# A decode attention kernel with gated MLP: thirty of its 32 units become a loop of 15 rounds

## The chip, the cores and the metric

The kernel runs on one core of one Trainium2 chip. A core has five engines with instruction streams of their own: TensorE (PE; its weight loads are shown as PEld), VectorE (DVE), ScalarE (ACT), GpSimd (POOL) and SyncE (SP), which here issues nearly all DMAs. The engines meet at semaphores. Sixteen DMA engines move the data. The metric is the device time in microseconds (us); before the change it is 1358.99, the median of three runs from 1357.01 to 1359.01.

## The reference

One token for each of two batches (B = 2, D = 1024). Attention has 32 heads of size 128 and a cache of 16384 positions; the MLP has F = 3584. All is bf16.

```python
g = sigmoid((x * gate_w).sum(-1, keepdims=True))
q = (x @ wq)                                  # 32 heads of 128
p = softmax((q @ k_cache^T) * Dh ** -0.5)     # by batch and head, over 16384 positions
a = (p @ v_cache) @ wo
h = gelu(layernorm(x) @ w1)
hs = shifted(h) @ w2                          # four column groups, shifted along the sequence
x1 = x + hs
b = x1 + gelu(layernorm(x1) @ w3) @ w4
out = g * a + (1 - g) * b
```

With a sequence of length one every shifted group is zero, so hs is zero; w2 is multiplied all the same. K and V caches are 537 MB together, the weights 36 MB.

## The kernel before

A unit is a pair of heads of one batch: 32 units, in the order of head pairs with the two batches inside. The K rows of a unit are 128 partitions of 256 positions of 128 values, 8.39 MB; V the same. One SBUF tile, mem, has five cells of half a unit each. K of even units lies in cells 0 and 1, K of odd units in cells 1 and 2, V in cells 3 and 4 (only unit 30's V lies in cells 0 and 1). So the next K may be loaded when the half unit in the cell that both share has been used.

For a unit n the loop at L599, written out by Python, does this:

- score_first(n) and score_second(n): eight chunks. VectorE turns a chunk (L464, KT, two buffers), then TensorE multiplies it in eight matmuls (L470) with a sliding window of q (qw) into one PSUM bank S. score_first takes the four chunks of the shared cell.
- load_k(n + 1) (L97) stands between the halves.
- softmax_a and softmax_b: turn S, the maximum, the exponentials in two halves on ScalarE (L509) into pt, the sum and its reciprocal.
- pv(n - 2): 64 matmuls (L542) in four groups of rows, from pt and V into oacc. So V lags K by two units, with four pt tiles.
- load_v(n - 1) (L100), which waits for pv(n - 2) to free the V cells.
- pv_end(n - 2): ScalarE scales oacc into osb, four small matmuls (L560) add the groups up into OT; after both batches of a head pair, wo_project multiplies with wo (L432). wo comes four heads at a time (L425) in 2 KB rows.

SyncE takes the DMAs in program order, each with its waits in front of it. In the steady state one load moves while the next stands in the queue or waits.

The MLP lies inside units 0 and 1: w1 and w2 are loaded to cells 2 and 3, w3 into 3 and 4, w4 likewise, each when the weight or the K before it has been used. Its activations are held turned (LinearT: wide_bank at L210 and then small matmuls at L241 and L275 that turn the result).

At the end, the V of unit 31 comes in 11 pieces (load_v_pieces, L108), so that pv_last can begin early: the first pieces as in pv, the rest position by position with V as the weights (L587). load_probes (L447) issues six tiny DMAs from gate_w into a tile that nothing reads; they write the same tile, so that each waits until the one before has landed, and they stand in SyncE's stream between the last loads of K and V. The result row goes out in two halves by the queues of SyncE and ScalarE.

Of the kernel before, what the change touches and what calls it, by code (L numbers as in the profile page):

```python
# [23 lines left out]
def kernel(  # L24
# [26 lines left out]

# [11 lines left out]
    assert NJ % CT == 0 and CT % GT == 0 and NG <= QP  # L63
# [3 lines left out]
    wopool = ctx.enter_context(tc.tile_pool(name="wopool", bufs=1))  # L67
# [3 lines left out]
    sps = ctx.enter_context(tc.tile_pool(name="sps", bufs=2, space=PSUM))  # L71
    ops = ctx.enter_context(tc.tile_pool(name="ops", bufs=1, space=PSUM))
    rps = ctx.enter_context(tc.tile_pool(name="rps", bufs=1, space=PSUM))
# [8 lines left out]
    def region(cell, elements):  # L82
        return mem[:, cell * CELL : cell * CELL + elements]

    k_cell = [0 if u % 2 == 0 else 1 for u in range(NU)]
    v_cell = [3] * NU
    v_cell[NU - 2] = 0
    units = [(hp, b) for hp in range(HP) for b in range(B)]

    def cache_rows(cache, u):  # L90
        hp, b = units[u]
        return cache[b, 2 * hp : 2 * hp + 2].rearrange("h s d -> (h s) d").rearrange(
            "(p j) d -> p (j d)", p=P
        )

    def load_k(u):
        nc.sync.dma_start(out=region(k_cell[u], NJ * Dh), in_=cache_rows(A_k_cache, u))  # L97

    def load_v(u):
        nc.sync.dma_start(out=region(v_cell[u], NJ * Dh), in_=cache_rows(A_v_cache, u))  # L100

    PIECES = [32] * 6 + [16] * 3 + [8] * 2
    assert sum(PIECES) == NJ

    def load_v_pieces(u):
        j = 0
        for n in PIECES:
            nc.sync.dma_start(  # L108
                out=region(v_cell[u], NJ * Dh)[:, j * Dh : (j + n) * Dh],
                in_=cache_rows(A_v_cache, u)[:, j * Dh : (j + n) * Dh],  # L110
            )
            j += n

    def k_view(u):
        return region(k_cell[u], NJ * Dh).rearrange("p (j d) -> p j d", d=Dh)

    def v_view(u):
        return region(v_cell[u], NJ * Dh).rearrange("p (j d) -> p j d", d=Dh)

    wq_t = region(3, KC * H * Dh).rearrange("p (r n) -> p r n", r=KC)  # L120
    nc.sync.dma_start(out=region(3, KC * H * Dh), in_=A_wq.rearrange("(p r) n -> p (r n)", p=P))
    xin = const.tile([P, B, KC], BF16)
    nc.sync.dma_start(out=xin[:], in_=A_x.rearrange("b s (p r) -> p (b s) r", p=P))
    gwT = const.tile([P, KC], BF16)
    nc.sync.dma_start(out=gwT[:], in_=gate_w.rearrange("(p r) -> p r", p=P))
    load_k(0)
# [12 lines left out]
    sel = const.tile([P, 4, Q4, QP], BF16)  # L139
    nc.gpsimd.memset(sel[:], 0.0)  # L140
    for v in range(4):
        w, e = divmod(v, 2)
        nc.gpsimd.affine_select(
            out=sel[:, v],
            in_=sel[:, v],
            compare_op=ALU.not_equal,
            fill=1.0,
            base=-(2 * QP * w + e),
            pattern=[[0, Q4], [-2, QP]],
            channel_multiplier=1,  # L150
        )
# [9 lines left out]
    )  # L161

# [11 lines left out]
    sel8 = const.tile([P, 8], FP32)  # L174
    nc.vector.tensor_reduce(
        out=sel8[:],
        in_=ident_f[:].rearrange("p (c k) -> p k c", k=QP)[:, 0:8, :],
        axis=AX.X,
        op=ALU.add,
    )  # L180
    oacc = [ops.tile([P, 4 * Dh], FP32, name=f"oacc{k}") for k in range(2)]
    for k in range(2):
        nc.vector.memset(oacc[k][:], 0.0)

    NW = 2
    WW = P + NG
    qw = []
    for k in range(NW):
        t = const.tile([P, 4, WW], BF16, name=f"qw{k}")
        nc.gpsimd.memset(t[:], 0.0)  # L190
        qw.append(t)
    NP = 4
    pts = []
    for k in range(NP):
        t = const.tile([P, NJ // 4, 2, 4], BF16, name=f"pt{k}")
        nc.gpsimd.memset(t[:], 0.0)
        pts.append(t)

    def copy_bank(j, dst, src):
        if j % 2 == 0:  # L200
            nc.scalar.activation(out=dst, in_=src, func=ACTF.Copy)  # L201
        else:
            nc.vector.tensor_copy(out=dst, in_=src)  # L203

    def wide_bank(j, actT, weight, R, dst):

        acc = oacc[j % 2]
        for r in range(R):
            q = r % Q4
            nc.tensor.matmul(  # L210
                acc[QP * q : QP * q + B, :],
                lhsT=actT[:, r, :],
                rhs=weight[:, r, :],
                start=(r < Q4),
                stop=(r >= R - Q4),
            )
        copy_bank(j, dst, acc[:])

    class LinearT:

        def __init__(self, W, actT, name, cell, offset):
            self.actT = actT
            K, self.N = W.shape
            self.R = K // P
            self.C = self.N // P
            self.src = W.rearrange("(p r) n -> p (r n)", p=P)
            at = cell * CELL + offset
            self.dst = mem[:, at : at + self.R * self.N]
            self.acc = mlp.tile([P, self.C, B], FP32, name=f"{name}_acc")

        def load(self):
            nc.sync.dma_start(out=self.dst, in_=self.src)

        def compute(self, wide):
            wc = self.dst.rearrange("p (r n) -> p r n", n=self.N)
            for j in range(self.N // 512):
                at = slice(j * 512, (j + 1) * 512)
                wide_bank(j, self.actT, wc[:, :, at], self.R, wide[:, at])
            ps = misc_psum([P, self.C, B])
            for c in range(self.C):  # L240
                nc.tensor.matmul(  # L241
                    ps[:, c, :],
                    lhsT=wide.rearrange("p (m c) -> p c m", c=self.C)[:, c, :],
                    rhs=sel8[:, 0:B],
                    start=True,
                    stop=True,
                )
            nc.vector.tensor_copy(out=self.acc[:], in_=ps[:])

    xn1T = mlp.tile([P, KC, B], BF16)  # L250
    hT = mlp.tile([P, KC, B], BF16)
    shT = mlp.tile([P, KC, B], BF16)
    x1T = mlp.tile([P, KC, B], FP32)
    xn2T = mlp.tile([P, KC, B], BF16)
    h2T = mlp.tile([P, FC, B], BF16)
    bT = mlp.tile([P, KC, B], FP32)

    lin1 = LinearT(B_w1, xn1T, "w1", 2, 0)
    lin2 = LinearT(B_w2, shT, "w2", 2, KC * D)
    lin3 = LinearT(B_w3, xn2T, "w3", 3, 0)  # L260
    lin4 = LinearT(B_w4, h2T, "w4", 3, 0)
    lin1.load()
    lin2.load()
# [3 lines left out]

    qps = misc_psum([P, H, B])
    HB = 512 // Dh
    qwide = mlp.tile([P, D], FP32, tag="wide", name="wide")[:].rearrange("p (t n) -> p t n", t=2)  # L270
    for j in range(H // HB):
        qo = qwide[:, j % 2]
        wide_bank(j, xT, wq_t[:, :, j * 512 : (j + 1) * 512], KC, qo)
        for k in range(HB):
            nc.tensor.matmul(  # L275
                qps[:, j * HB + k, :],
                lhsT=qo[:, k * Dh : (k + 1) * Dh],
                rhs=sel8[:, 0:B],
                start=True,
                stop=True,  # L280
            )
    lin3.load()
    qT = const.tile([P, H, B], BF16)
    nc.vector.tensor_copy(out=qT[:], in_=qps[:])
    qdps = misc_psum([P, 4, H * B])
    for v in range(4):
        nc.tensor.matmul(
            qdps[:, v, :],
            lhsT=sel[:, v].rearrange("p a k -> p (a k)"),
            rhs=qT[:].rearrange("p h b -> p (h b)"),  # L290
            start=True,
            stop=True,
        )

    qd = const.tile([P, HP, B, 4], BF16)
    for e in range(2):
        rows = slice(e * HALF, (e + 1) * HALF)
        nc.vector.tensor_copy(
            out=qd[rows],
            in_=qdps[rows].rearrange("p v (hp e b) -> p hp e b v", e=2, b=B)[:, :, e],  # L300
        )
    qdu = qd[:].rearrange("p hp b v -> p (hp b) v")

    def write_qw(u):
        t = qw[u % NW]
        dst = t[:, :, NG - 1 : NG - 1 + QP * (Q4 - 1) + 1 : QP]
        nc.gpsimd.tensor_tensor(  # L307
            out=dst,
            in0=qdu[:, u, :].unsqueeze(2).to_broadcast([P, 4, Q4]),
            in1=mask4[:].unsqueeze(1).to_broadcast([P, 4, Q4]),  # L310
            op=ALU.mult,
        )

    g_rep = const.tile([P, B], FP32)

    def compute_gate():
        xg = mlp.tile([P, B, KC], FP32, name="xg")
        nc.vector.tensor_tensor(
            out=xg[:], in0=xin[:], in1=gwT[:].unsqueeze(1).to_broadcast([P, B, KC]), op=ALU.mult
# [57 lines left out]
    def wide4():  # L377
        return mlp.tile([P, D], FP32, tag="wide", name="wide")[:]
# [298 lines left out]
```

## Time and profile before

| what | value |
|---|---|
| three runs, us | 1357.01 to 1359.01, median 1358.99 |
| profiled execution, first to last instruction, us | 1358.0 |
| bytes read from HBM | 572.53 MB, 422 GB/s over the span |
| mean granted TensorE clock | 0.785 |
| K or V of one unit | 8.39 MB, 64 such in all |
| VectorE turning K chunks (L464) | 571.4 us in 256 instructions of 2.28 us |
| TensorE scores (L470) | 551.9 us in 2048 matmuls |

A window's line has its start and end, its length, then busy time and number of instructions of PE, PEld, DVE, ACT and POOL, then the granted clock, the share of the 16 DMA engines' time that packets took, and GB/s; packets are counted where they start. In the table of SyncE's waits, a line names the issuing line, who released it, the total, how often, and the longest. In the timeline a row has start and length, engine, line, operation and tiles, how many, and in brackets the idle time before it and who ended it. SPq marks an instruction of SyncE's stream that issues a DMA.

### The profile page before, as it was taken

Reading aid. Unit: us, or ns where it says so; the run is one execution under the profiler, and the core shown is the slowest. Engines: PE = TensorE matmul, PEld = TensorE weight load, DVE = VectorE, ACT = ScalarE, POOL = GpSimd, SP = SyncE. Lnnn points to the kernel's source line nnn. Section 1 sums busy time; section 2 is a strip of 40 time slices with the busy share of each in tenths; the row PEclk is TensorE's granted clock in tenths of the full one; section 3 lists DMA queues with packets and bytes.
Section 4 is the critical chain, followed back from the end, with each engine's and each line's share of the span. In section 5 each row is a group of like instructions: output and inputs, shape, how many; then the busy total and the mean of one; then the engine's idle time right before and its main releaser. Section 6 shows DMA issues by size and latency. Waiting matters only on the chain.

```text
span 1358.0 us, 11505 instructions
## 1 busy us (share of the span) xinstructions
PE 806.9 (59%) x5086; PEld 366.8 (27%) x5086; DVE 650.4 (48%) x511; ACT 133.5 (10%) x208; POOL 15.2 (1%) x54
## 2 busy tenths in 40 slices
PE   2897855555665545566555556655456665555564
PEld 1463422222222222222222222222222222222222
DVE  1436654444555534455544445555344555444450
ACT  0011011111100111110011111001111100111110
POOL 1000000000000000000000000000000000000000
PEclk9977877778876768888777788877678886777886
DMA  9987999999999999999999999999999999999996
GB/s 402 433 360 315 431 433 433 431 431 427 433 433 432 424 438 433 435 435 426 436 433 433 431 429 433 431 431 428 433 431 429 433 427 432 435 435 435 425 424 277
DMA packets 16183, 573.26 MB, mean 422 GB/s; under 512 B 1922, under 2 KB 1926, under 8 KB 6662
## 3 DMA queue, kind: packets, MB, share of 16 engines
q1 hardware_dynamic: 16130, 572.54, 98.1%
q8 instruction: 39, 0.64, 0.2%
q14 instruction: 10, 0.08, 0.0%
q10 hardware_dynamic: 4, 0.00, 0.0%
HBM read 572.53 MB, written 0.00 MB: 422 GB/s over the span
## 4 chain that ended last, share of the span: by engine, by line
DMA 67%; PE 17%; DVE 12%; issue 3%; ACT 0%; SPq 0%; POOL 0%; DVEq 0%; ACTq 0%
DMA mem<-in_A_k_cache_dram 57%; PE S L470 12%; DVE KT L464 11%; DMA probe<-in_gate_w_dram 7%; PE misc L241 2%; DMA xin<-in_A_x_dram 2%; PE oacc L210 1%; PE misc L275 1%; DMA wo<-in_A_wo_dram 1%; DMA mem<-in_A_v_cache_dram 0%; PE oacc L542 0%; PE arow L409 0%; ACT pt L509 0%; ACT mem L201 0%; DVE wide L203 0%
## 5 line engine op out<-in xcount | busy, mean ns | idle before, releaser
L470 PE MATMUL S<-KT,qw 128*128 128x512 bf16 x2048 | 551.9, 420 | 385.0 <-DVE KT L464 384.6
L464 DVE STREAM_TRANSPOSE KT<-mem 128x2048 f32<-128x2048 f32 x256 | 571.4, 2283 | 297.3 <-DMA mem<-in_A_k_cache_dram 243.6
L470 PEld LDWEIGHTS <-qw 128*128 128x128 bf16 x2048 | 219.8, 108 | 711.0 <-issue 537.0
L542 PE MATMUL oacc<-mem,pt 128*8 128x512 bf16 x2008 | 115.5, 382 | 8.6 <-DMA mem<-in_A_v_cache_dram 8.6
L495 ACT ACTIVATE Dm<-ident_s,m 128x128 f32<-128x128 f32 x32 | 12.8, 401 | 983.6 <-DVE m L493 983.6
L509 ACT ACTIVATE pt<-St,nb 64x256 bf16<-64x256 f32 x64 | 89.7, 1402 | 73.3 <-DVE nb L507 65.7
L572 DVE TENSOR_SCALAR OT<-misc,g_rep 128x2 bf16<-128x2 f32 x31 | 6.9, 222 | 140.5 <-PE misc L560 140.5
L520 PE MATMUL misc<-rs,lmat 128*128 128x1 f32 x62 | 17.8, 356 | 87.0 <-ACT pt L509 87.0
L542 PEld LDWEIGHTS <-pt 128*8 128x8 bf16 x2008 | 46.2, 87 | 74.5 <-issue 23.6
L522 DVE RECIPROCAL rinv<-misc 128x1 f32<-128x1 f32 x31 | 5.2, 168 | 101.6 <-PE misc L520 101.6
L491 DVE STREAM_TRANSPOSE St<-S 128x512 f32<-128x512 f32 x32 | 22.9, 717 | 63.7 <-PE S L470 63.7
L560 PE MATMUL misc<-sel,osb 128*128 128x2 f32 x256 | 34.5, 257 | 26.7 <-ACT osb L555 26.7
L560 PEld LDWEIGHTS misc<-sel,osb 128*128 128x128 f32 x256 | 31.8, 195 | 42.9 <-ACT osb L555 42.9
L520 PEld LDWEIGHTS misc<-rs,lmat 128*128 128x128 f32 x62 | 15.1, 303 | 97.9 <-ACT pt L509 97.7
L509 ACT ACTIVATION_READ_ACCUMULATOR pt<-St,nb 64x1 f32 x64 | 30.6, 478 | 0.0
L555 ACT ACTIVATE osb<-oacc,rinv 128x512 f32<-128x512 f32 x31 | 21.3, 687 | 69.0 <-PE oacc L542 69.0
L210 PE MATMUL oacc<-mem,xT 128*2 128x512 bf16 x64 | 9.4, 612 | 24.0 <-DVE xT L266 23.2
L307 POOL TENSOR_TENSOR qw<-qd,mask 128x16 bf16<-128x16 bf16 x32 | 8.4, 266 | 1180.9 <-PE S L470 1137.3
L507 DVE TENSOR_REDUCE nb<-misc 64x1 f32<-64x64 f32 x64 | 14.2, 222 | 5.0 <-PE misc L501 0.9
L275 PEld LDWEIGHTS misc<-sel,wide 128*128 128x128 f32 x64 | 14.2, 328 | 7.4 <-issue 4.4
L203 DVE COPY wide<-oacc 128x512 f32<-128x512 f32 x7 | 4.8, 691 | 22.9 <-PE oacc L210 22.9
L501 PE MATMUL misc<-Dm,ones_f 128*128 128x128 f32 x64 | 15.6, 326 | 0.0
(96 smaller groups left out, 168.3 us busy)
## 6 DMA issues: line engine op xcount, KB each, us to landing
mem<-in_B_w_dram SPq DMA_DIRECT2D x2, 7168.0 KB, 25.0
wo<-in_A_wo_dram SPq DMA_DIRECT2D x7, 1024.0 KB, 32.8
mem<-in_A_v_cache_dram SPq DMA_DIRECT2D x6, 1024.0 KB, 5.9
mem<-in_B_w_dram SPq DMA_DIRECT2D x2, 2048.0 KB, 45.9
mem<-in_A_v_cache_dram SPq DMA_DIRECT2D x3, 512.0 KB, 14.3
wo<-in_A_wo_dram SPq DMA_DIRECT2D x2, 512.0 KB
mem<-in_A_k_cache_dram SPq DMA_DIRECT2D x32, 28.2
mem<-in_A_v_cache_dram SPq DMA_DIRECT2D x2, 256.0 KB, 14.0
```

The source lines that it names most:

```text
L210: nc.tensor.matmul(acc[QP * q : QP * q + B, :], lhsT=actT[:, r, :], rhs=weight[:, r, :], start=(r < Q4), stop=(r >= R - Q4),)
L241: nc.tensor.matmul(ps[:, c, :], lhsT=wide.rearrange("p (m c) -> p c m", c=self.C)[:, c, :], rhs=sel8[:, 0:B], start=True, stop=True,)
L275: nc.tensor.matmul(qps[:, j * HB + k, :], lhsT=qo[:, k * Dh : (k + 1) * Dh], rhs=sel8[:, 0:B], start=True, stop=True,)
L464: nc.vector.transpose(out=kt[:], in_=Kc.rearrange("p j d -> p (j d)").bitcast(FP32))
L470: nc.tensor.matmul(S, lhsT=t[:, v, NG - 1 - m : NG - 1 - m + P], rhs=ktb[:, half * GT : (half + 1) * GT, w, :, e], start=(first and n == 0 ...
L491: nc.vector.transpose(out=st[:].rearrange("p j r -> p (j r)"), in_=S[:])
L501: nc.tensor.matmul(R_ps[:], lhsT=ones_f[:], rhs=Dm[:], start=True, stop=True)
L509: nc.scalar.activation(out=Pt[rows, :, e, :].rearrange("p (m a) k -> p a k m", a=GT // 4), in_=st[rows, :, 0:NG].rearrange("p (a k) m -> p ...
L520: nc.tensor.matmul(tot_ps[:, 0:1], lhsT=lmat[:], rhs=rs[:], start=True, stop=True)
L542: nc.tensor.matmul(acc[QP * q : QP * q + 8, :], lhsT=pts[u % NP][:, g].rearrange("p h k -> p (h k)"), rhs=v_view(u)[:, 4 * g : 4 * g + 4, ...
L555: nc.scalar.activation(out=osb[:], in_=oacc[u % 2][:], func=ACTF.Copy, scale=rinvs[u % NP][:, 0:1] if scaled else 1.0,)
L560: nc.tensor.matmul(ot[:], lhsT=osb[:, k * Dh : (k + 1) * Dh], rhs=sel8[:, k : k + 5 : 4], start=(k == 0), stop=(last and k == 3),)
```

## The change

1. The MLP comes first, ahead of the scores, with w1, w2, w3 and wq loaded at once into free cells, K of unit 0 after w3 has been used, and w4 in V's cells. x and gate_w are loaded by ScalarE's queue. The matmuls of the MLP and of q run as four column groups (rows4), and VectorE turns the results.
2. V lags K by one unit, so that two pt tiles suffice: K(n + 1), V(n), K(n + 2), V(n + 1).
3. wo is loaded and multiplied by head pairs (load_wo, project), 4 KB a row; pv_end sums into the layout that fits it, in sixteen small matmuls. arow takes one PSUM bank in four row groups.
4. The probes go. The last V comes in five pieces, and into cells 0 and 1.
5. Units 1 to 30 become a hardware loop of 15 rounds (from the second half of an odd unit to the first half of the next one). The addresses of the loads come from the loop's register. Its semaphores are not set back between rounds; they grow, and the waits compare with registers that grow by the same amount every round. The last unit stands in a branch inside the loop that only round 14 takes. The instruction order shows what the other rounds run instead: an arm that adds to each engine's and each load's semaphore what the last unit would have added. Before each such addition stands a wait for the count that the semaphore must have by then. On SyncE these are the counts of the round's two K loads, two V loads and the wo pair.

```diff
+    xin = const.tile([P, B, KC], BF16)
+    nc.scalar.dma_start(out=xin[:], in_=A_x.rearrange("b s (p r) -> p (b s) r", p=P))
...
+    w1 = load_weight(B_w1, 0)
+    w2 = load_weight(B_w2, 0, KC * D)
+    w3 = load_weight(B_w3, 1)
+    wq = load_weight(A_wq, 3)
+
+    K_CELL = (0, 1)
+    V_CELL = 3
+
+    def cache_rows(cache, hp, b):
+        two = cache[b, bass.ds(2 * hp, 2)]
+        return two.rearrange("h s d -> (h s) d").rearrange("(p j) d -> p (j d)", p=P)
...
+    def rows4(acc, actT, weight, R, at, n, G):
         for r in range(R):
+            for g in range(Q4):
+                nc.tensor.matmul(
+                    acc[QP * g : QP * g + B, 0:n],
+                    lhsT=actT[:, r, :],
+                    rhs=weight[:, r, g * G + at : g * G + at + n],
+                    start=(r == 0),
+                    stop=(r == R - 1),
                 )
...
+    def load_wo(hp):
+        rows = A_wo[bass.ds(hp * 2 * Dh, 2 * Dh)]
+        nc.sync.dma_start(
+            out=wo_pair[:].rearrange("p t n -> p (t n)"),
+            in_=rows.rearrange("(p t) n -> p (t n)", p=P),
+        )
+
+    def project(oT, weight, last):
+        for t in range(2):
+            for g in range(Q4):
+                nc.tensor.matmul(
+                    arow[QP * g : QP * g + B, :],
+                    lhsT=oT[:, t, :],
+                    rhs=weight[:, t, g * G1 : (g + 1) * G1],
...
-    def load_probes():
-        for n, pitch, width in (
-            (17, 60, 20), (2, 512, 30), (4, 256, 40), (8, 128, 50), (11, 93, 60), (13, 78, 70),
-        ):
...
+    def pv_end(b):
+        osb = pv_rows(b, True)[:].rearrange("p (k d t) -> p k t d", k=4, t=2)
+        ot = misc_psum([P, 2])
+        for t in range(2):
+            for k in range(4):
+                for h in range(2):
+                    nc.tensor.matmul(
+                        ot[h * HALF : (h + 1) * HALF, t : t + 1],
+                        lhsT=osb[:, k, t, :],
+                        rhs=lane[:, k + 4 * h : k + 4 * h + 1],
...
+    PIECES = (128, 64, 32, 16, 16)
...
+    load_k(0, 0)
+    w4 = load_weight(B_w4, 3)
+    score_first(0, 0)
+    load_k(0, 1)
+    score_second(0)
+    softmax_a(0)
+    mlp_last(w4)
+    load_v(0, 0)
+    softmax_b(0)
+
+    def odd_rest(hp):
+        load_k(hp + 1, 0)
+        score_second(1)
+        softmax_a(1)
+        pv(0)
+        load_v(hp, 1)
+        pv_end(0)
+        softmax_b(1)
+
+    def even_unit(hp):
+        score_first(hp, 0)
+        load_k(hp, 1)
+        score_second(0)
+        softmax_a(0)
+        pv(1)
+        load_v(hp, 0)
+        pv_end(1)
+        project(oT, wo_pair, False)
+        load_wo(hp)
+        softmax_b(0)
+        score_first(hp, 1)
+
+    load_wo(0)
+    score_first(0, 1)
+
+    def last_unit(hp):
+        V_LAST = 0
+        load_v(hp, 1, V_LAST, PIECES)
+        score_second(1)
+        wo_last = region(V_CELL, 2 * D).rearrange("p (h n) -> p h n", h=2)
+        softmax_a(1)
+        pv(0)
+        pv_end_apart(0)
+        nc.sync.dma_start(
+            out=wo_last, in_=A_wo[(H - 2) * Dh : H * Dh].rearrange("(h d) n -> d h n", d=Dh)
+        )
+        softmax_b(1, by_head=True)
+        pv_last(1, V_LAST)
+        project(OTl, wo_last, True)
...
+        with tc.For_i(0, HP - 1, 1, iteration_sync="reg_based") as i:
+            odd_rest(i)
+            even_unit(i + 1)
+            with tc.If(i >= HP - 2):
+                last_unit(HP - 1)
```

## The prediction

> **What bounds the kernel now.** I read four views. First the page: engines at half load, DMA at nine tenths in nearly every slice.
>
> ```profile
> PE 806.9 (59%) x5086; PEld 366.8 (27%) x5086; DVE 650.4 (48%) x511; ACT 133.5 (10%) x208; POOL 15.2 (1%) x54
> DMA  9987999999999999999999999999999999999996
> GB/s 402 433 360 315 431 433 433 431 431 427 433 433 432 424 438 433 435 435 426 436 433 433 431 429 433 431 431 428 433 431 429 433 427 432 435 435 435 425 424 277
> ```
>
> So time is bytes over rate plus the places where the stream breaks. Second the windows (last two columns: share of the 16 DMA engines, GB/s), which price the breaks:
>
> ```profile
> 0.00:140.00 140.00, 98.45 (x522) 59.60 (x522) 53.51 (x80) 11.93 (x21) 7.76 (x26) 0.88 0.89 375
> 140.00:1320.00 1180.00, 691.91 (x4296) 296.66 (x4295) 595.25 (x425) 118.21 (x182) 7.47 (x28) 0.78 1.00 432
> 1320.00:1340.00 20.00, 8.41 (x99) 3.91 (x99) 0.85 (x4) 2.77 (x6) 0.00 (x0) 0.67 0.77 313
> ...
> 68.00:70.00 2.00, 2.00 (x10) 2.00 (x10) 0.92 (x1) 0.00 (x0) 0.00 (x0) 0.95 0.04 8
> 70.00:72.50 2.50, 2.50 (x15) 1.07 (x15) 0.89 (x3) 0.60 (x1) 0.00 (x0) 0.50 0.00 0
> 72.50:75.00 2.50, 2.50 (x7) 0.81 (x6) 0.24 (x2) 0.00 (x0) 0.00 (x0) 0.50 1.29 419
> ...
> 114.00:122.50 8.50, 7.86 (x28) 2.92 (x27) 7.03 (x4) 0.00 (x0) 0.00 (x0) 0.79 0.00 0
> ```
>
> From 140 to 1320 us the stream never breaks: 432 GB/s. It breaks at the start (first packet at 1.8), near 70 and 114 us (the queue runs dry) and in the last 38 us. Third, SyncE's waits: K's load waits for the transposes that free its half cell, and the probes wait for each other.
>
> ```profile
> SPq L97 <- DVE KT L464: 351.8, 31, 28.5
> SPq L447 <- DMA probe<-in_gate_w_dram: 36.3, 5, 14.6
> ```
>
> Fourth the timeline, one unit and the first dry spot: how long after K has landed the next K is issued (11.2 us; the V behind it moves for 19.4), and how soon after an issue bytes flow (issue 71.72, above nothing until 72.5).
>
> ```profile
> 1249.59 4.50 DVE L464 STREAM_TRANSPOSE KT<-mem 128x2048 f32<-128x2048 f32 x2 [7.74 <-DMA mem<-in_A_k_cache_dram]
> ...
> 1260.74 0.33 SPq L97 DMA_DIRECT2D mem<-in_A_k_cache_dram  x1
> ...
> 71.72 0.33 SPq L97 DMA_DIRECT2D mem<-in_A_k_cache_dram  x1
> ```
>
> **The change, part by part.** One K or V load is 8.39 MB, so 19.4 us at 432 GB/s.
>
> Front. The breaks at 70 and 114 us come from K loads that wait for MLP work. 0 to 140 us at 375 instead of 432 GB/s costs 140 x (1 - 375/432) = 18.5 us; of it the start keeps 1.8 idle and 0.95 for slow first packets (first 64 KB packets took about 3.2 us, later ones 2.42, and began up to 0.2 apart): 2.7. The new order loads w1, w2, w3, wq (19.9 MB, done near 49 us) with x and gate_w on ACT's own queue. Work in that cover: gate and layer norm took 48.2 to 52.7 us here, 4.5 us; two small layers with gelu about 10; w3's 64 matmuls, in 16 groups at the cold 0.43 us, 7. From w3's landing near 29 us this ends by 37, and K0 is not due before 49. The rest: w4 waits for wq's matmuls (49 + 7 = 56, due 68); K1 for 11.2 us after K0 (80, due 85); V0 for w4's 112 matmuls after unit 0's scores (about 96, due 104); K2 for unit 1's first half (about 118, due 124). Nothing breaks: -15.8 us. If x came late behind weight packets, K0 still has 12 us of cover. Of the front's matmuls none is on the path.
>
> Probes. 1320 to 1340 us at 313 GB/s costs 5.5, by the DMA share of 0.77 4.6: the last V pieces stand behind probes that wait for their predecessor to land. The probes go: -5. The end after the last packet (1353.45 to 1358.0) stays, with the same piece matmuls, projection, copy and store; leaving the loop adds a wait row and a barrier on each engine, +1 (0.4 to 2; the barrier rows at the end of this trace last 0.6).
>
> wo. Heads 30 and 31 are loaded twice (as a pair in round 14, then apart): 0.52 MB, +1.2 us. Pairs come as 4 KB rows. Each single-buffered pair waits for its predecessor's projection, which ends some 10 us after the V load ahead of it starts; that V covers it. The eight matmuls of a projection are spread over 15 rounds, PE idle 41%: nothing. Sixteen small fp32 matmuls a unit replace four, which are eight rows of 0.12 us here (0.97 us a unit): 3 us more of PE. After the odd unit's V that makes 7 for pv, 1 for the copy, 4, 1 for the projection and about 5 of softmax, 18 us, ahead of the next K at 19.4; a few us late would only use up the 6 that PE has before the drain. Nothing, but this is the thinnest cover.
>
> K and V in turn. V(n) now follows K(n+1) and not K(n+2); pv(n) reads it one unit later. V's cell must be free 19.4 us after pv's data landed. In the order of the changed kernel pv of the even unit is mixed with the second score half: from V's landing 3.6 us of pv (64 matmuls), 32 score matmuls at 0.24, a cold start: 14 us. The odd unit's pv stands after all eight chunks: about 26 us after K, 7 after V landed. Both have 5 to 10 us left: nothing, and if that cover fell short by a microsecond it would cost 15.
>
> The loop. Semaphores are counted so that every round adds the same, whether or not the arm of the last round ran. In the rounds that skip it an else-arm makes up the counts, and each engine first waits for its own counts. PE, DVE and ACT wait for what they have done anyway. SyncE's arm, as the built order shows, waits for the landing of every load of the round, V and wo pair too, and only then may it pass on to the next round's K. Before, that K was issued with a V still moving (1260.74 above). So in 14 rounds (the last takes the true arm) the DMA queue runs empty: V, wo pair, nothing behind.
>
> What does one drain cost? Idle: from the last packet to SyncE's next issue 0.65 us (five probes: 0.52 to 0.75 from their last packet to the next issue); about 14 sequencer instructions of SyncE between (rest of the arm, two branches, counters, five waits) at 0.06 us, the spacing of the met waits at this trace's end: 0.84; from issue to first packet 0.97 (71.72 to 72.69; 121.69 to 122.66). Sum 2.5. Edges: the 18.5 us above less 13.0 idle (1.8, 2.67 from 70.02 to 72.69, 8.51) leave 5.5 for three slow starts of 0.95 and two run-outs, in which some of the 16 engines finish up to 1.9 us before the last: 1.3 each. One drain has one of both: 2.3. Together 4.8 us, and 14 drains 67 us. Loop branches and waits on registers are not in this trace. Low: 0.5 + 0.4 + 0.9 idle, edges 1.5, so 3.3. High: four of the 14 as long as SyncE's longest row, 0.5, idle 4.0, edges 2.7 as near 70 us, so 6.7. I take 4.8: the two dry spots are the same event. 14 drains: 46 to 94 us.
>
> The Trainium skill ("DMA: Bandwidth & Descriptors", Anatomy of one DMA) gives each transfer about 2.0 us that do not scale with its bytes. By it 14 drains would be 28 us and the time 1368; the dry spot near 70 us, 2.67 us idle and some 2 more in edges, speaks for more.
>
> Sum against the profiled execution: 1358.0 - 15.8 - 5 + 1.2 + 1 + 67 = 1406.4. The median of the runs, 1358.99, is 1.0 above that span, so 1407.
>
> **Rivals.** (1) Faster: the drain is nearly free. Without it the sum is 1358.0 - 15.8 - 5 + 2.2 + 1 = 1340. It decides at (1359 - 1340)/14 = 1.3 us a round: under that the kernel is faster. For it: the last load of a round is small (0.5 MB), and if its packets filled the gaps of engines that finish early, the run-out would vanish. Against: issue to first packet alone is 0.97 and the notice 0.5. Time 1345 to 1359. (2) A light drain, 1.3 to 3.3 us: 1359 to 1386. (3) The edge costs more: SyncE's jumps over the true arm and back wait for code. A tiny transfer's full round (stores issued 1355.6, waited for until 1356.98) is 1.3 us, an 8 KB code packet took 0.3 to 0.55; some 1.9 a jump, two a round: 14 x 3.8 = 53 more, 1460. For it: every other part of the loop is new. Against: SyncE's loop is some 70 instructions, less than one such packet. The Trainium skill ("Runtime: NRT & Kernel Launch", Instruction fetch mechanics) has a taken branch out of the fetched window wait for its page; no loop runs in this trace. For PE, whose round is nearly 600 instructions and whose jump skips 450 more, stalls of up to 6 us hide before the V it waits for, 10 more behind the next K. (4) Compute becomes late: pv after V's landing takes over 20 instead of 14 us, or the chain of small matmuls holds up the next scores, and SyncE waits for PE in each round; each microsecond costs 15: 1420 to 1450. Against: the 10 us left.
>
> **How the numbers follow.** Forecast (3.3 to 6.7 a drain) 0.78; (1) 0.05; (2) 0.06; (3) 0.06; (4) 0.05. Likeliest 1407. The forecast's own range is 1386 to 1434; with 3 us for the front and tail, and reaching into (3) and (4), 1383 to 1440. A measurement here can tell about 0.2%, 2.7 us. Only (1) is not slower: faster 0.04, same 0.01, slower 0.95.
>
> **What would show it.** Right: the DMA row between 5 and 1330 us has 14 dry spots of 2 to 4 us, some 80 to 85 us apart, each after a wo pair's landing and ended by a K issue; none before 120 us; SyncE's longest waits name V or wo landings at the loop's end; 432 GB/s between. Wrong: no dry spots (1), spots of 1 us (2), spots over 5 us (3), K or V issues released by PE with the queue empty (4), or a dry spot before 120 us (front).

## The result and the profile after

The changed kernel takes 1401.1 us (median of four runs, 1400.64 to 1401.93) against 1359.0 for the kernel before on the same chip (1357.01 to 1359.68): a ratio of 1.0315, 95% interval 1.030 to 1.033. The profiled execution took 1400.64 us, its span is 1398.5. The forecast was 1407.

The page of the changed kernel: its span, the DMA and GB/s rows in 40 slices of 35 us, and the queue that fetches code.

```profile
span 1398.5 us, 14865 instructions
DMA  9999989989899998999989999998999999998995
GB/s 420 396 442 432 428 376 442 427 375 444 381 422 427 396 450 375 429 396 420 450 375 441 384 420 405 420 450 375 424 399 422 403 422 420 405 420 379 446 420 241
q8 instruction: 8, 0.13, 0.0%
```

The hole near 110 us is gone; instead slices of 375 to 396 GB/s recur to the end. The windows put prices on it (last columns: granted clock, DMA share, GB/s):

```profile
0.00:140.00 140.00, 58.54 (x571) 26.36 (x575) 52.97 (x83) 8.07 (x15) 5.34 (x19) 0.83 0.99 422
140.00:1320.00 1180.00, 695.97 (x4798) 289.56 (x4787) 572.82 (x403) 112.99 (x174) 7.49 (x28) 0.78 0.96 413
1320.00:1384.00 64.00, 37.93 (x288) 15.65 (x289) 26.08 (x24) 7.79 (x12) 0.00 (x0) 0.78 1.00 426
1384.00:1398.50 14.50, 7.09 (x115) 4.14 (x107) 0.59 (x2) 0.60 (x1) 0.00 (x0) 0.62 0.01 2
```

The front went from 375 to 422 GB/s. The long middle went from 432 to 413: 1180 x (1 - 413/431.9) = 52 us. And the kernel now runs 14 us on after its last large packet, where before it ran 4.5.

The middle holds 14 dry spots, the first at 207.30 us, the others 82.3 to 82.9 us apart, each of 2.62 to 2.74 us without any packet. The first one, 206 to 212 us in 40 slices of 0.15 us (packets are counted where they start):

```profile
DMA  4444332000000000000000000099990999000000
GB/s 164 191 191 164 164 137 82 27 0 0 0 0 0 0 0 0 0 0 0 0 0 0 0 0 0 0 2621 437 1748 437 0 437 874 437 0 0 0 0 0 0
```

The small packets at the left are the rows of the wo pair; the large ones at the right are the next round's K, issued by SyncE 1.73 us after the last packet of wo (timeline):

```profile
209.03 0.33 SPq L108 DMA_DIRECT2D mem<-in_A_k_cache_dram  x1
```

SyncE's waits name the place: L632 is the branch that holds the last unit; 42 waits are three in each of 14 rounds. The table names the branch itself as the releaser, because each of these instructions raises the semaphore that it waits for. Which landing ends each wait shows in the trace's times: in the first round the three waits end at 187.1, 206.5 and 207.7 us, each within 0.05 us of the last landing of the round's second K, its second V and its wo pair. Only what follows the last of them stops the stream; the two before run while data still moves.

```profile
SPq L632 <- SPq L632: 413.6, 42, 19.4
```

The end of the kernel, TensorE from 1352 us on and then the last burst:

```profile
1353.53 1.90 PE L426 MATMUL S<-KT,qw 128*128 128x512 bf16 x8 [0.30 <-DVE KT L420]
1362.38 1.87 PE L492 MATMUL oacc<-mem,pt 128*8 128x512 bf16 x13 [6.95 <-DMA mem<-in_A_v_cache_dram]
1364.17 4.62 PE L426 MATMUL S<-KT,qw 128*128 128x512 bf16 x16
...
1389.02 2.30 PEld L548 LDWEIGHTS <-mem 128*128 128x128 bf16 x64
1389.13 2.27 PE L548 MATMUL misc<-pt,mem 128*128 128x2 bf16 x64
1393.15 0.16 DVE L552 TENSOR_TENSOR OTl<-misc,rinv 128x2 bf16<-128x2 f32 x1 [10.07 <-remote]
```

TensorE stands still for 6.95 us for the V of the other batch (pv(0)) while scores of the last unit that could run are queued behind it. And VectorE starts 1.75 us after the last matmul of the burst has ended. Neither was in the prediction.

Theories. T1: the else-arm's wait for landings on SyncE empties the DMA queue in 14 rounds, and that is the whole loss in the middle. T2: the loop's machinery as such costs it (branches, waits against registers, a semaphore raise on each TensorE instruction). T3, narrower: branch and arm cost the time whatever they wait for. For the end: the order of TensorE's work in the last unit.

### The profile page after: what moved, and what is told of

Same layout as the page of the kernel before. It is cut to its first block, busy times and chain, and to the rows that moved or that the text cites. A ratio compares the mean times of both kernels' runs of the same rounds, so it can differ in the third digit from the quotient of the medians.

```text
span 1398.5 us, 14865 instructions
## 1 busy us (share of the span) xinstructions
PE 799.5 (57%) x5758; PEld 335.7 (24%) x5758; DVE 652.5 (47%) x511; ACT 129.4 (9%) x202; POOL 12.8 (1%) x47
## 2 busy tenths in 40 slices
DMA packets 13529, 573.20 MB, mean 410 GB/s; under 512 B 1864, under 2 KB 1872, under 8 KB 4432
## 5 line engine op out<-in xcount | busy, mean ns | idle before, releaser
L426 PE MATMUL S<-KT,qw 128*128 128x512 bf16 x2048 | 564.8, 429 | 301.6 <-DVE KT L420 295.1
L492 PE MATMUL oacc<-mem,pt 128*8 128x512 bf16 x2032 | 146.0, 408 | 113.8 <-SPq L632 96.3
L492 PEld LDWEIGHTS <-pt 128*8 128x8 bf16 x2032 | 50.1, 88 | 197.1 <-issue 153.4
L525 DVE TENSOR_SCALAR oT<-misc,g_rep 128x2 bf16<-128x2 f32 x30 | 6.7, 222 | 120.2 <-PE misc L517 120.2
L517 PE MATMUL misc<-lane,osb 128*64 128x1 f32 x960 | 33.8, 199 | 39.4 <-ACT osb L505 39.4
L517 PEld LDWEIGHTS misc<-lane,osb 128*64 128x64 f32 x960 | 31.7, 138 | 54.1 <-ACT osb L505 28.1
L357 POOL TENSOR_TENSOR qw<-qdu,mask 128x16 bf16<-128x16 bf16 x32 | 8.5, 267 | 1239.9 <-PE L492 1165.2
L462 DVE TENSOR_REDUCE nb<-misc 64x1 f32<-64x64 f32 x64 | 14.2, 222 | 9.3 <-PE misc L457 5.2
L449 DVE TENSOR_REDUCE m<-St 128x1 f32<-128x256 f32 x32 | 13.4, 420 | 1.1
L457 PEld LDWEIGHTS misc<-Dm,ones_f 128*128 128x128 f32 x64 | 9.9, 195 | 0.7 <-issue 0.2
```

The costliest lines, as they stand in the source:

```text
L426: nc.tensor.matmul(S, lhsT=qw[b][:, v, NG - 1 - m : NG - 1 - m + P], rhs=ktb[:, half * GT : (half + 1) * GT, w, :, e], start=(first and n ...
L449: nc.vector.tensor_reduce(out=m[:], in_=st[:, :, 0:NG], axis=AX.XY, op=ALU.max)
L457: nc.tensor.matmul(R_ps[:], lhsT=ones_f[:], rhs=Dm[:], start=True, stop=True)
L462: nc.vector.tensor_reduce(out=nb[rows], in_=R_ps[rows, rows], axis=AX.X, op=ALU.min)
L492: nc.tensor.matmul(oacc[b][QP * q : QP * q + 8, :], lhsT=pts[b][:, g].rearrange("p h k -> p (h k)"), rhs=V[:, 4 * g : 4 * g + 4, :].rearra ...
L517: nc.tensor.matmul(ot[h * HALF : (h + 1) * HALF, t : t + 1], lhsT=osb[:, k, t, :], rhs=lane[:, k + 4 * h : k + 4 * h + 1], start=(k == 0 a ...
```

## The experiments

Each run is compared with runs of the kernel before on its own chip; those had medians of 1356.8 to 1357.8 us.

| run | us | ratio to before, 95% |
|---|---|---|
| rounds written out | 1343.47 | 0.9893 (0.9878 to 0.9908) |
| last unit behind the loop | 1346.66 | 0.9919 (0.9904 to 0.9934) |
| before, without probes | 1356.63 | 0.9994 (0.9985 to 1.0003) |
| V last in the round | 1402.39 | 1.0329 (1.0314 to 1.0345) |
| three pieces | 1347.91 | 0.9923 (0.9905 to 0.9940) |
| four pieces | 1383.42 | 1.0183 (1.0165 to 1.0201) |
| order of the last unit | 1397.29 | 1.0290 (1.0271 to 1.0308) |
| three pieces and order | 1343.07 | 0.9884 (0.9867 to 0.9902) |
| the same, short last burst | 1341.03 | 0.9879 (0.9863 to 0.9896) |
| behind the loop, and order | 1348.82 | 0.9941 (0.9924 to 0.9957) |
| written out, and order | 1343.61 | 0.9901 (0.9885 to 0.9918) |

### The rounds written out

```diff
-    LOOPED = True
+    LOOPED = False
```

> The changed kernel with its fifteen rounds written out one behind the other: no loop, no branch, no growing semaphores, every load and every edit of the change otherwise kept. Theory T1 (the else-arm's waits for landings drain the DMA stream once a round, 14 times, about 3.7 us each by bytes, 52 us in all): no dry spot behind 120 us, and 1401 - 52 = 1349 us, up to 4 us less if the tail's late semaphore notices go too: 1345 to 1350. It is then 9 to 14 us faster than the kernel before. Theory T2 (the loop's machinery as a whole costs the time: branches on every engine, waits against registers, a semaphore increment on every TensorE instruction) expects the same 1345 to 1350, so this run does not tell the two apart; it tells both from the theory that one of the other edits (the alternation of K and V, the wo pairs, the 16 small matmuls behind each unit) carries the loss, which expects 1385 to 1400.

1343.47 us, no dry spot between the start and 1338 us. The page of this run, the DMA row and the queue that fetches code:

```profile
DMA  9999999999999999999999999999999999999997
q8 instruction: 45, 0.74, 0.2%
```

So all other parts of the change together make the kernel 14 us faster, and the loop takes 58 back. Of these the drains are 52; the other 5.5 lie in the end (below).

### The last unit behind the loop

```diff
             even_unit(i + 1)
-            with tc.If(i >= HP - 2):
-                last_unit(HP - 1)
+        last_unit(HP - 1)
```

> The changed kernel with the same loop of fifteen rounds, register waits and growing semaphores, but without the arm: the last unit stands behind the loop, so that SyncE has no else-arm and nothing in a round that waits for the round's landings. T1: no dry spot inside the loop, one at its exit of 2.5 to 4 us; 1401 - 52 + 4 for the exit = 1353 us, range 1343 to 1357. T2 (the loop itself): the stream still stops or slows once a round, 1390 to 1402. In between (1360 to 1385) each would hold a part.

1346.66 us. The loop with its register waits and semaphore raises is still there, and the middle (window and page of this run) is whole:

```profile
140.00:1300.00 1160.00, 714.48 (x4957) 295.58 (x4948) 586.52 (x414) 116.89 (x180) 7.49 (x28) 0.78 1.00 433
```

```profile
DMA  9999999999999999999999999999999999999986
```

The only dry spot is at the loop's exit, 2.03 us at 1307.6. T2 falls: the loop itself costs the stream nothing that shows. It even helps a little: by the bytes from 140 to 1300 us this kernel moves 433.1 GB/s, the one with its rounds written out 431.7, with the same 4 KB rows of wo. There 47 code packets (queues q8 and q14) take 2.7 us of the sixteen engines' time in this stretch, here one takes 0.06.

### Three pieces

The DMAs of the rounds and of the arm take eight completion semaphores in turn, as the instruction order and the trace show: a round uses five (numbers 0 to 4: K, V, K, V, wo), the arm the next ones. Five pieces of V, the last wo and the two result rows make eight, so the arm comes round to numbers 0 to 4, and the else-arm, which must raise them, first waits for what the round has loaded on them. With three pieces it stops at number 2.

```diff
-    PIECES = (128, 64, 32, 16, 16)
+    PIECES = (128, 64, 64)
```

> The changed kernel with loop and arm kept; only the last unit's V comes in three pieces instead of five. SyncE's loads take eight completion semaphores in turn; a round takes five (K, V, K, V, wo pair), the arm then takes the next ones. With five pieces the arm's loads and stores reach round to the semaphores of this round's V and wo, and the else-arm, which has to raise each of the arm's semaphores in its place, waits for these landings. With three pieces it reaches only as far as the round's second K, whose landing lies some 20 us of stream ahead of wo's. Theory T1 in this form (the drain is the wait for the last landings, nothing else of the arm): no dry spot in any round, 1401 - 52 = 1349 us, range 1345 to 1353, with the late tail of the changed kernel still in it. Rival T3 (the branch and the arm cost the time by themselves, whatever they wait for): 1395 to 1402 with the 14 dry spots.

1347.91 us, inside the range of T1. SyncE's waits and the windows of this run:

```profile
SPq L632 <- SPq L632: 119.9, 15, 9.1
```

```profile
0.00:140.00 140.00, 59.25 (x567) 26.23 (x571) 52.85 (x83) 8.19 (x15) 5.33 (x19) 0.84 0.99 424
140.00:1310.00 1170.00, 719.33 (x4976) 299.80 (x4969) 591.65 (x417) 116.86 (x180) 7.48 (x28) 0.78 1.00 433
```

SyncE still waits at L632 in every round, up to 9.1 us, but for a K with 20 us of stream behind it: the wait is covered and costs nothing. T3 falls too. A number in a list of piece sizes, in a part that runs once, cost 53 us.

### Four pieces

```diff
-    PIECES = (128, 64, 32, 16, 16)
+    PIECES = (128, 64, 32, 32)
```

> As the run with three pieces, with four: the else-arm now waits as far as the round's second V, and only the wo pair (0.52 MB, 1.2 us of stream) may still be under way when SyncE goes on. T1: SyncE's way from V's landing to the first packet of the next K stays 2.7 us, of which wo covers 1.2: each drain costs 1.2 us less, 3.7 - 1.2 = 2.5 us, 14 of them 35 us, 1401 - 17 = 1384 us, range 1379 to 1389, with dry spots of 1.3 to 1.6 us. T3: 1395 to 1402, dry spots unchanged. If a drain costs only when the stream is quite dry: the same 1384.

1383.42 us: 0.6 from what was expected. The 14 dry spots are 1.32 to 1.52 us long, as the 1.2 us of wo behind the awaited V says they should be, and SyncE has two waits a round instead of three. The same spot, 206 to 212 us:

```profile
DMA  4443210000000000099999000000000000000999
```

```profile
SPq L632 <- SPq L632: 395.6, 28, 19.6
```

```profile
140.00:1310.00 1170.00, 705.39 (x4887) 293.99 (x4883) 578.54 (x408) 113.38 (x175) 7.75 (x29) 0.78 0.98 420
```

So the price goes with how much stream lies behind the awaited landing: 0, 1.2 and 20 us of it give drains of 3.7, 2.4 (33.7 us in 14 by bytes) and 0 us.

### V last in the round

```diff
         pv(1)
-        load_v(hp, 0)
         pv_end(1)
         project(oT, wo_pair, False)
         load_wo(hp)
+        load_v(hp, 0)
```

> The changed kernel with one line moved: in every round the wo pair is issued ahead of the even unit's V instead of behind it, so that the last packets ahead of each drain are V's instead of wo's rows of 4 KB. This tests the term that the prediction mis-sized: the edges of a drain, taken at 2.3 us and measured at 1.1. If the run-out of large packets is what makes an edge long, each of the 14 drains costs 0.8 to 1.1 us more: 1412 to 1417 us. If the edges do not hang on what comes last: 1400 to 1403 us.

1402.39 us, and again 14 dry spots, of 2.59 to 2.79 us:

```profile
140.00:1310.00 1170.00, 688.10 (x4777) 286.82 (x4766) 563.91 (x401) 112.99 (x174) 7.48 (x28) 0.78 0.96 412
```

The run-out (the time lost while some of the 16 engines have finished and others have not) does not hang on the size of the last packets: from the bytes of the 10 us ahead of a spot, against 431.9 GB/s, it costs 0.42 us in the changed kernel and 0.39 here, as means over 14 spots. So wo's small packets do not explain why it is small. The traces show what does go with it: the first of the 14 spots costs 1.1 to 1.2 us in all four kernels that have them, the later ones 0.1 to 0.8, and the one stop at the exit of the loop without an arm, after some 1300 us without any, costs 1.2. The two spots at the front of the kernel before, with 1.6 and 1.05, are like a first stop and not like those of later rounds. Why a later run-out is smaller was not tried.

### The kernel before without its probes

```diff
-            if n == NU - 3:
-                load_probes()
```

> The kernel before without its probe loads, which nothing reads (that is all that it leaves out). The prediction put them at 5 us; by the bytes the stretch of 1320 to 1340 us lost 4.9 us in the kernel before and the like stretch of the changed one 0.5. If the probes are that loss: 1354 to 1355 us, 4 to 5 us below the kernel before. If the loss belongs to the run-out of the stream and not to the probes: 1358 to 1359.

1356.63 against 1357.32 us: 0.7 less, by the interval between 2.0 less and 0.4 more, so no gain that can be told from none. Yet the stretch that lost the bytes is mended in the profiled execution (the last column, GB/s, was 313 before):

```profile
1320.00:1340.00 20.00, 9.95 (x125) 5.42 (x126) 0.85 (x4) 2.47 (x4) 0.00 (x0) 0.67 0.98 411
```

Those two profiled spans differ by 3.0 us, but 1.7 of these also lie between the two series of the kernel before (medians 1359.0 where it was profiled, 1357.3 beside this run). Of each only one execution was profiled, so what the probes cost as a rule is open. What stands is that the 5 us of the prediction were read from one execution and are at most 2.

### The order of the last unit

```diff
         softmax_a(1)
-        pv(0)
+        last = softmax_b(1, by_head=True)
+        with tc.issue_after(last.ins):
+            pv(0)
         pv_end_apart(0)
...
-        softmax_b(1, by_head=True)
         pv_last(1, V_LAST)
```

(softmax_b returns its last matmul here.)

> The changed kernel, rounds and drains as they are; in the last unit all scores and the softmax are put ahead of the unit's pv of the other sequence, so that TensorE does not wait for that V (7 us idle from 1355.4 us on) with the scores behind it. Theory on the tail (the last unit's own chain is late, by TensorE's order): the end comes 4 to 6 us behind the last packet of V instead of 14.3, so 1401 - 8 = 1393 us, range 1391 to 1396. Rival (the end is late because TensorE's 128 semaphore increments in the last burst are taken up at 30 ns each, 1.7 us late, or because the landing of the last V is): 1398 to 1401.

1397.29 us: 3.8 less, half of what was expected. The chain of this run shows where the other half went:

```profile
1372.05 0.58 PE oacc L493
1372.63 0.52 PE misc L482 x2
1373.15 5.52 PE oacc L493 x58
1378.67 0.69 ACT osb L506
```

The softmax is done some 13 us earlier (its last exponentials end at 1368.5 us instead of 1381.4). TensorE goes on behind it only 9.4 us earlier, at 1372.05 instead of 1381.50, when the first piece of the last V has landed. And pv(0), which filled gaps among the scores, now stands between the softmax and the last unit's own pv: 5.5 us of the gain pay for it.

### Three pieces and the order

The two edits above in one kernel.

> Three pieces and the last unit's order together, loop and arm kept. If both theories hold and the two add: 1401 - 52 - 8 = 1341 us, range 1338 to 1345, 14 to 20 us below the kernel before and level with the unrolled form of the change (1343.5). If the tail is hidden or bound otherwise once the drains are gone: 1346 to 1350. If the drains stay: 1390 to 1395.

1343.07 us; the order is worth 4.8 here, and the drains stay away. With loop and arm it is level with the rounds written out.

### A shorter last burst

In the kernel of the section before, with its order:

```diff
-    PIECES = (128, 64, 64)
+    PIECES = (192, 48, 16)
```

> The kernel with three pieces and the last unit's order, with the pieces cut as 192, 48 and 16 rows instead of 128, 64 and 64: the last burst on TensorE is 16 weight loads and 16 matmuls instead of 64 and 64. In the loop each TensorE instruction raises a semaphore; VectorE's multiply behind the burst started 1.74 us after the burst's end in the two kernels with 64 pairs, though it waits for nothing else. If these raises are taken up one by one at 30 ns (128 of them 3.84 us against 2.1 to 2.3 us of burst), 32 of them take 0.96 us against 0.57 us: the gap falls to 0.4 us, give or take 0.15. If the gap is a fixed price of a wait inside the arm: it stays at 1.6 to 1.8 us. Time: 1343 less 1.3 (gap) and less 0.8 to 1.7 (burst, less what the 12 more moving matmuls take): 1340 to 1341.5 us by the first, 1341.5 to 1343 by the second.

1341.03 us, the lowest of all times and 4% below the changed kernel. Against the kernel with pieces of 128, 64 and 64 the gain is not settled by the times: the ratios to the kernel before, 0.9879 and 0.9884, lie within each other's intervals; on this run's chip the kernel before was 1.0 us faster as well. The gap itself shows in the timeline:

```profile
1332.10 0.56 PEld L549 LDWEIGHTS <-mem 128*128 128x128 bf16 x16
1332.21 0.54 PE L549 MATMUL misc<-pt,mem 128*128 128x2 bf16 x16
1333.35 0.16 DVE L553 TENSOR_TENSOR OTl<-misc,rinv 128x2 bf16<-128x2 f32 x1 [7.30 <-PE misc L549]
```

The burst ends at 1332.75, VectorE starts 0.60 later instead of 1.74: a little over the range of the first theory (0.25 to 0.55), far from a fixed price. From the burst's first weight load to VectorE's start it is 1.25 us for 32 raises (1332.10 to 1333.35) and 4.13 us for 128 (1389.02 to 1393.15 above), so 2.88/96 = 30 ns a raise and 0.29 us besides. The times of TensorE's semaphore in the trace show the same without a fit: in the changed kernel 129 raises stand 30 ns apart from 1389.285 to 1393.125 us, 1.73 us past the last matmul, and VectorE starts at 1393.15. With the last unit behind the loop, where TensorE's instructions do not raise one by one, the same 64 pairs leave no gap:

```profile
1335.55 1.77 PE L548 MATMUL misc<-pt,mem 128*128 128x2 bf16 x64
1337.36 0.16 DVE L552 TENSOR_TENSOR OTl<-misc,rinv 128x2 bf16<-128x2 f32 x1 [7.79 <-PE misc L548]
```

There the 64 pairs also take 1.77 us instead of 2.27.

### The order, where nothing is late

The same order in the loop without an arm, and with all rounds written out.

> The loop without an arm (last unit behind the loop) and the last unit's order as in the run of that alone. The last unit's instructions are then outside the loop, so that TensorE raises no semaphore per instruction there: the gap behind the last burst is 0.1 us or less. The order took 4.1 us off the changed kernel and 4.8 off the one with three pieces; if it takes as much here: 1346.7 - 4.5 = 1342 us, range 1340 to 1344. If the wait for the loop's exit (a dry spot of 2.0 us) sets the last V's landing and with it the end: 1344 to 1346.7.

1348.82 us: 2.2 slower than without the order (3.0 by the ratios, whose intervals just touch), outside both expectations. The traces agree: from V's last packet to the end it is 14.4 us here and 9.6 without the order. Its chain:

```profile
1328.19 6.05 PE oacc L493 x62
1334.24 0.02 issue
1334.27 0.70 ACT osb L506
1334.96 0.04 issue
1335.01 1.05 PE misc L559 x8
1336.06 2.07 PE oacc L493 x35
```

At the loop's exit (dry spot at 1307.7) the V of pv(0) has landed: without the order pv(0) starts at once there, at 1308.70 us. So TensorE had nothing to stall on; the order only moves 6 us of matmuls behind the softmax.

> All rounds written out, and the last unit's order. In the unrolled form the end already comes 3.6 us behind the last packet, so the last unit's chain is not late there and the order has nothing to give: 1342.5 to 1344.5 us, as without it. If the order is worth the same 4 us there: 1339 to 1340.

1343.61 against 1343.47 us: no change, as expected where the end already comes 3.6 us after the last packet.

## Why the prediction was right, and where it was off

**What bounds the kernel.** Right. In every run time is bytes over 431.7 to 433.6 GB/s plus the stops of the stream and the end after it.

**Front, -15.8.** Right in mechanism and size: against 431.9 GB/s the first 140 us lost 19.0 us before and 4.35 after, -14.7, and no dry spot lies ahead of 207 us.

**Probes, -5.** Mis-sized: 0.7 (up to 2.0) where it was tried alone. The account of the written-out kernel agrees, though it is no test of a term this small: -14.7 for the front, +1.2 for wo and -0.7 make -14.2; measured -13.9.

**wo by pairs, +1.2.** The 0.52 MB are there, but the bytes in all did not grow (573.26 MB before, 573.20 after): the loop fetches 0.5 MB less code. From 10 us behind a drain to 10 us ahead of the next the rate is 433.6 GB/s, against 431.8 in the middle of the kernel before. The larger wo rows do not do that, since the written-out kernel has them and moves 431.7; it goes with the loop, whose missing code packets (2.3 us of the sixteen engines' time from 140 to 1300 us in the kernel before, 0.2 in the changed one) are the likely reason for half of it or more. The prediction had no term for this gain of 3 to 5 us.

**V one unit closer, and pv_end's sixteen small matmuls, nothing.** Right: with three pieces nothing stops the stream from 140 to 1310 us, so the thin cover holds.

**The loop.** Place, count, spacing and the landings that are waited for were as forecast, though SyncE's table names the branch where the prediction expected V or wo; three pieces, four pieces and the unit behind the loop show that the else-arm's landing waits are the cause. The price of a drain was the mis-sized term, 4.8 us against 3.7, 67 us against 52. By parts, the first three measured on the first spot (the others are within 0.1 of it), the last two as means over all 14:

| part | predicted | measured |
|---|---|---|
| last packet to SyncE's notice | 0.65 | 0.38 |
| SyncE's instructions to the K issue | 0.84 | 1.35 |
| issue to first packet | 0.97 | 0.96 |
| run-out of the 16 engines | 1.3 | 0.42 |
| slow first packets | 0.95 | 0.84 |

The idle part was right within 0.2 us, with luck: two errors partly cancel, the notice too long and SyncE's 14 instructions, rightly counted, too short at 0.06 us each where they take about 0.1. The step that failed is "the two dry spots are the same event": the run-out, taken from the front's two spots, was three times too long, and only the first drain has one of that kind (1.1 us). The parts sum to 3.95; by bytes against 431.9 GB/s it is 3.72, since the stream between is a little faster. The Trainium skill ("DMA: Bandwidth & Descriptors", Anatomy of one DMA) has about 2.0 us fixed for a transfer on GpSimd's path. The prediction put that on SyncE's loads, and 14 of these gave 1368 us. The trace differs: 2.69 us without a packet, 1.35 of it SyncE's own instructions between two transfers, and 1.3 in the edges.

**The end, "stays", +1 for the exit.** This step failed. From 1320 us on the stream and what follows it lose 11.5 us before and 14.9 after, against 431.9 GB/s: +3.5 where probes and end together were put at -4. Against the written-out kernel the changed one's end is some 6 us late (57.6 us in all less 52.1 for the drains are 5.5; by the bytes from 1320 us on it is 6.6), for two reasons that the runs show: pv(0) waits for a V that comes one unit later and, in the arm, ahead of scores that could run (the order gave 3.8 to 4.8 us back), and the raises at 30 ns each delay the last notice by 1.75. I had looked at what the end computes, not at the order in which TensorE does it now. That 1407 is only 6 us above the measured 1401 is luck: 15 us too much for the drains hide 7.5 too little for probes and end and 1 too little for the front.

**Rivals.** (1) and (2) fall, 3.7 us is over their bounds, though with four pieces a drain of 2.4 us does give a time in the range of (2). (3), code fetched at the loop's edge: the whole run has 8 code packets of 0.13 MB, and none in the loop's last 14 rounds, so this loop, with 672 matmuls and weight loads a round, is not fetched again. Nothing here speaks for the wait for code behind a taken branch (the Trainium skill, "Runtime: NRT & Kernel Launch", Instruction fetch mechanics) at these branches. (4) falls with the stream at 433 GB/s.

## What to carry to other kernels

When a loop keeps counts that every round must match, look up what the branch not taken waits for: here the else-arm that raised a load's semaphore waited for that load, and with as many DMAs in the arm as there are semaphores it waited for everything that was just issued. A wait for a landing was free with 20 us of stream queued behind what it awaits and not with 1.2; by the length of the dry spots some 2.7 us and the run-out would be needed, which no run tried. With none behind it, the notice, the issuing engine's instructions and the issue-to-packet time are paid in every round. Reorder an end only where the trace shows an engine waiting: the same order was worth 4 to 5 us, nothing, and -2 to -3 us in kernels that differ only in what is late.

## What the runs showed of the hardware that I had not expected

Where each TensorE instruction raises a semaphore, the raises are taken up one per 30 ns: 64 weight loads and 64 matmuls that ran in 2.4 us are noticed 4.13 us after they began, 16 and 16 after 1.25. It showed where a dense burst of short instructions was the last thing that somebody waited for. The first packets after each stop took 3.1 us on average instead of 2.42 and began 0.3 to 1.2 us apart, which together make the 0.84 us of slow start at every drain, in the loop as at the kernel's front. And the run-out ahead of a stop cost 1.05 to 1.6 us at the front and at a loop's first stop, but 0.1 to 0.8 us where the stream had stopped one round before.
